# The linear factor of a cubic moved from VectorE to GpSimd, behind a wait, in an attention and rational-activation kernel

## The chip, the cores and the metric

One core of a Trainium2 chip. The metric is the device time of one execution in microseconds (us); three executions of the kernel before took 319.7, 320.22 and 322.7 us, the median is 320.22 us. Its engines are named as in the profile: PE is the matrix engine (PEld its weight loads), DVE is VectorE, ACT is ScalarE, POOL is GpSimd, SP issues DMAs.

## The reference

Two stages. The first is an attention with features of a polynomial sketch (4 batches, 4 heads, 1088 tokens, head width 32, 8 sketch rows); the second is a layer with a rational activation, from 128 to 2048 and back to 128, over all 4352 tokens.

```
def phi(x):                       # 8 x 8 = 64 features of each token
    a = einsum('rd,bhsd->bhsr', S1, x);  b = einsum('rd,bhsd->bhsr', S2, x)
    return einsum('bhsi,bhsj->bhsij', a, b).reshape(..., 64)
kv = einsum('bhsf,bhsd->bhfd', phi(k), v);   z = sum over s of phi(k)
x  = (phi(q) @ kv) / (phi(q) . z + 1e-6)     # heads joined: 4352 x 128

h = x @ w_in                                  # 4352 x 2048
P = a[0] + a[1]*h + a[2]*h*h + a[3]*h*h*h     # the cubic
Q = 1 + |b[0]|*|h| + |b[1]|*h*h
out = (P / (Q + 1e-6)) @ w_out                # 4352 x 128, float32
```

## The kernel before, in words

The attention of batch 0 begins by itself (lines 447 to 475); the rest of the attention is cut into tasks (lines 488 to 498), and one task is mixed into each step of the main loop (line 527) until the last query piece is done. A task is the keys of one batch (class Keys) or a piece of up to 256 tokens of queries (class Queries: transposes, sketches, copies, features, products, quotient, back, keep). Keys and queries use PE, a copy on ACT, and on DVE the features (an operand in PSUM, lines 203, 276 and 279), the quotient (lines 294 to 297) and transposes.

The activation works on units (lines 322 to 332): 512 tokens by 4 blocks of 128 hidden columns, that is a tile of 128 x 2048; the first two units are 256 tokens by 8 blocks, the last two are half as wide (128 x 1024). There are 35 units, NU. For unit i, with h in bf16 as hh:

- PE: hidden(i, 0) and hidden(i, 1), line 356, four float32 products each into a PSUM tile h_ps (two buffers)
- ACT: evac(i, 0) and evac(i, 1), line 364, PSUM to hh (four buffers)
- DVE: d_abs, u = |hh| by a mask (line 368); d_w, w = |b1|*u + |b0| (line 373, a scaling); d_y, y = w*u (line 378, a product); d_p, p = a3*hh + a2 (line 382, a scaling: the linear factor of the cubic)
- ACT: a_ln, ln = Ln(y + 1 + 1e-6) (line 387); a_exp, r = Exp(-ln) = 1/Q (line 391)
- DVE: d_s, s = hh*r (line 395); d_hs, hs = hh*s (line 399); d_g, g = p*hs (line 403): three products
- PE: gather, line 421, adds r, s and g times three copies of w_out (one scaled by a[0], one by a[1], one plain) in PSUM; so out = a0*r + a1*s + g, times w_out
- store, line 432, when a chunk of tokens is complete: a DVE transpose of PSUM, then DMAs on SP's queue

Nothing reorders the work: the kernel is under a manual schedule, and each engine does its instructions in the order in which the loop writes them; tiles carry the waits between engines. Step i of the loop works on several units at once: hidden and evac on unit i + 2, d_abs, d_w, d_y and d_p on unit i, a_ln and a_exp on unit i - 1, d_s, d_hs and d_g on unit i - 2, gather on unit i - 3, store on unit i - 4. In step i VectorE's order before is (lines 540 to 568):

```
s(i-2), u(i), store's transpose, hs(i-2), key and query features,
w(i), g(i-2), more key features, y(i), p(i), quotient, transposes of the next task
```

GpSimd has no instruction in the loop: it sets constants at the start (lines 116 to 128) and makes the plain bf16 copy of w_out (line 523).

Of the kernel before, what the change touches and what calls it, by code (L numbers as in the profile page):

```python
# [14 lines left out]
AX = mybir.AluOpType  # L15
# [5 lines left out]
def kernel(  # L21
# [13 lines left out]
    nc = tc.nc  # L35
# [23 lines left out]
    mid = ctx.enter_context(tc.tile_pool(name="mid", bufs=2))  # L59
    late = ctx.enter_context(tc.tile_pool(name="late", bufs=3))  # L60
# [77 lines left out]
    for i in range(2):  # L138
        nc.vector.tensor_mul(out=S12[:, :, i, :],
                             in0=sT[i][:, None, 0:R].broadcast_to([128, H, R]),  # L140
# [11 lines left out]
    ab0, ab1 = b_abs[:, 0:1], b_abs[:, 1:2]  # L152
    a2, a3 = a_sb[:, 2:3], a_sb[:, 3:4]
# [179 lines left out]
    live = [dict() for _ in range(NU)]  # L333
    outs = {}

    def ok(i):
        return 0 <= i < NU

    def width(i):
        return units[i][1] * units[i][3]  # L340

    def new(i, key, pool, dt=BF, bufs=None):
        kw = {} if bufs is None else {"bufs": bufs}
        t = pool.tile([128, UW], dt, name=key, **kw)[:, 0:width(i)]
        live[i][key] = t
        return t

    def hidden(i, part):
        if not ok(i) or part * HW >= width(i):
            return  # L350
        t0, tl, f0, per = units[i]
        assert ready[0] >= t0 + tl
        t = live[i]["h", part] = wide()
        for x in range(HW // tl):
            f = f0 + part * (HW // tl) + x
            nc.tensor.matmul(t[:, x * tl:(x + 1) * tl], lhsT=w_in_sb[:, f * 128:(f + 1) * 128],  # L356
                             rhs=xT[:, t0:t0 + tl], start=True, stop=True)

    def evac(i, part):
        if not ok(i) or part * HW >= width(i):  # L360
            return
        if part == 0:
            new(i, "hh", late, bufs=4)
        nc.scalar.copy(out=live[i]["hh"][:, part * HW:(part + 1) * HW], in_=live[i]["h", part])  # L364

    def d_abs(i):
        if ok(i):
            nc.vector.tensor_scalar(out=new(i, "u", mid, bufs=1).bitcast(U16), in0=live[i]["hh"].bitcast(U16),  # L368
                                    scalar1=0x7FFF, scalar2=None, op0=AX.bitwise_and)

    def d_w(i):
        if ok(i):
            nc.vector.tensor_scalar(out=new(i, "w", mid, bufs=1), in0=live[i]["u"], scalar1=ab1, scalar2=ab0,  # L373
                                    op0=AX.mult, op1=AX.add)

    def d_y(i):
        if ok(i):
            nc.vector.tensor_mul(out=new(i, "y", mid), in0=live[i]["w"], in1=live[i]["u"])  # L378

    def d_p(i):  # L380
        if ok(i):
            nc.vector.tensor_scalar(out=new(i, "p", mid), in0=live[i]["hh"], scalar1=a3, scalar2=a2,  # L382
                                    op0=AX.mult, op1=AX.add)

    def a_ln(i):
        if ok(i):
            nc.scalar.activation(out=new(i, "ln", mid, FP, bufs=1), in_=live[i]["y"], func=ACT.Ln, bias=1.0 + 1e-6)  # L387

    def a_exp(i):
        if ok(i):  # L390
            nc.scalar.activation(out=new(i, "r", late), in_=live[i]["ln"], func=ACT.Exp, scale=-1.0)  # L391

    def d_s(i):
        if ok(i):
            nc.vector.tensor_mul(out=new(i, "s", late), in0=live[i]["hh"], in1=live[i]["r"])  # L395

    def d_hs(i):
        if ok(i):
            nc.vector.tensor_mul(out=new(i, "hs", mid, bufs=1), in0=live[i]["hh"], in1=live[i]["s"])  # L399

    def d_g(i):
        if ok(i):
            nc.vector.tensor_mul(out=new(i, "g", late), in0=live[i]["p"], in1=live[i]["hs"])  # L403
# [3 lines left out]
    def gather(i, part):  # L407

        if not ok(i):
            return  # L410
        t0, tl, f0, per = units[i]
        if f0 == 0 and part == 0:
            pool = att if t0 >= n_tok - 3 * TC else ops
            outs[t0] = pool.tile([128, TC], FP, name="att_ps" if pool is att else "out_ps")
        order = [(x, y) for x in range(per) for y in range(3)]
        if i == NU - 1:
            order = [(x, y) for y in range(3) for x in range(per)]
        n = len(order)
        for x, y in order[n * part // 4:n * (part + 1) // 4]:
            f = f0 + x  # L420
            nc.tensor.matmul(outs[t0][:, :tl], lhsT=w_sb[y][:, f, :],  # L421
                             rhs=live[i][KEYS[y]][:, x * tl:(x + 1) * tl],
                             start=(f == 0 and y == 0), stop=(i == NU - 1 or units[i + 1][0] != t0) and (x, y) == order[-1])

    def store(i):
        if not ok(i):
            return
        t0, tl, f0, per = units[i]
        if f0 + per < nf:
            return  # L430
        o = mid.tile([128, TC], FP, name="out_sb")
        nc.vector.transpose(out=o[:, :tl], in_=outs[t0][:, :tl])
        c = t0
        while c < t0 + tl:
            b = c // S
            ce = min(t0 + tl, (b + 1) * S)
            o_b = out[b * S:(b + 1) * S, :].rearrange("(g j) d -> g j d", g=32)
            j0, j1 = (c - b * S) // 32, (ce - b * S) // 32
            for e in range(d_model // 32):
                eng = nc.scalar if i == NU - 1 and e % 2 else nc.sync  # L440
                eng.dma_start(
                    out=o_b[:, j0:j1, e * 32:(e + 1) * 32],
                    in_=o[e * 32:(e + 1) * 32, c - t0:ce - t0].rearrange("p (j d) -> p j d", d=32))
            c = ce
# [36 lines left out]
    def fetch(b):  # L481
        fetched[b] = (load_k(b), load_v(b), load_q(b))
# [19 lines left out]
    def get_keys(b):  # L502
        if b is None:
            return Nothing()
        if b not in keys:
            keys[b] = Keys(b, fetched[b][0], fetched[b][1])
        return keys[b]

    def get_queries(bx):
        if bx is None:  # L510
            return Nothing()
        if bx not in pieces:
            b, x = bx
            pieces[bx] = Queries(b, fetched[b][2] if b else q0, cuts[x], cuts[x + 1])
        return pieces[bx]

    def weights():
        nc.scalar.activation(out=b_abs, in_=b_sb, func=ACT.Abs)
        for f in range(0, nf, 4):
            for y in range(2):  # L520
                nc.vector.tensor_scalar(out=w_sb[y][:, f:f + 4], in0=w_out_sb_f[:, f:f + 4],
                                        scalar1=a_sb[:, y:y + 1], scalar2=None, op0=AX.mult)
            nc.gpsimd.tensor_copy(out=w_sb[2][:, f:f + 4], in_=w_out_sb_f[:, f:f + 4])
# [3 lines left out]
    for i in range(-2, NU + 4):  # L527
        kb, kc, qx = tasks.get(i, none)
        KB, KC, Q = get_keys(kb), get_keys(kc), get_queries(qx)
        P = get_queries(tasks.get(i - 1, none)[2])  # L530
        if i in fetch_at:
            fetch(fetch_at[i])

        KC.products((0, 1))
        KB.sketches(0)
        KB.sketches(1)
        Q.sketches()

        a_ln(i - 1)
        d_s(i - 2)  # L540
        d_abs(i)
        KC.keep()
        KB.copies(0)
        KB.copies(1)
        Q.copies()
        store(i - 4)
        hidden(i + 2, 0)
        P.back()
        d_hs(i - 2)
        KB.features(0)  # L550
        Q.features()
        d_w(i)
        a_exp(i - 1)
        P.keep()
        hidden(i + 2, 1)
        d_g(i - 2)
        KB.features(1)
        Q.products()
        d_y(i)
        evac(i + 2, 0)  # L560
        for part in range(4):
            gather(i - 3, part)
        evac(i + 2, 1)
        d_p(i)
        Q.quotient()
        nk, _, nq = tasks.get(i + 1, none)
        get_keys(nk).transposes()
        get_queries(nq).transposes()
        if i == -1:
            weights()  # L570
# [31 lines left out]
```

## Time and profile before

| | before |
|---|---|
| median of three executions | 320.22 us (319.7 to 322.7) |
| the profiled execution's own time | 322.05 us |
| its span, first to last instruction | 320.1 us, 3822 instructions |
| PE busy | 286.5 us, 90% |
| PEld busy | 152.6 us, 48% |
| DVE busy | 282.3 us, 88% |
| ACT busy | 216.2 us, 68% |
| POOL busy | 4.2 us, 1%, 24 instructions |
| DMA | 11.29 MB, 35 GB/s over the span |
| mean granted clock of PE | 0.962 |

The profile is of one execution. Busy time is the union of an engine's instructions; instructions of one engine can overlap by some hundredths of a us at their ends, so what one costs in a row of many is read from start to start. In a row of groups stand line, engine, operation, what is written and read with its shape, the count, the busy time and the mean in ns, then the idle time ahead of them and what ended it. A row of stages gives start and end, the length, and then busy time and count. The chain of work that ended last is followed back from the last instruction to what released each.

### The profile page before, as it was taken

What the parts mean: (1) busy time and instruction counts of PE and PEld (TensorE: products, weight loads), DVE (VectorE), ACT (ScalarE), POOL (GpSimd) and SP (SyncE); (2) the same over time, 40 slices, a digit from 0 to 9 for tenths busy, and PEclk for the clock granted to TensorE, in tenths of its full rate; (3) what the DMA queues carried; (4) which work ended last, traced back from release to release, by engine and by line L of the source; (5) the groups of instructions that cost most, each with busy time, mean ns of one, the idle gap of its engine ahead of it and who ended that gap; (6) DMA issues with size and microseconds to landing.
All of it is one profiled execution on the core that took longest, in us unless ns stands there. A gap on an engine that the chain in (4) does not pass through costs nothing.

```text
span 320.1 us, 3822 instructions
## 1 busy us (share of the span) xinstructions
PE 286.5 (90%) x1420; PEld 152.6 (48%) x1420; DVE 282.3 (88%) x410; ACT 216.2 (68%) x226; POOL 4.2 (1%) x24
## 2 busy tenths in 40 slices
PE   0969769979999999999999999999999899995763
PEld 0857635646655555554565555444433343342221
DVE  2430299799999999999999999999999999999992
ACT  1123454877786688778667778887888878887450
POOL 2020000000000000000000000000000000000000
PEclk9996997979999999999999999999999999999589
DMA  5894020000080002000100001001000100200202
GB/s 176 281 257 112 0 73 0 0 3 0 15 212 1 2 0 33 3 0 0 31 3 2 0 9 25 2 0 32 3 2 4 28 0 0 33 2 0 33 1 33
DMA packets 24626, 11.29 MB, mean 35 GB/s; under 512 B 20384, under 2 KB 22432, under 8 KB 24608
## 3 DMA queue, kind: packets, MB, share of 16 engines
q1 hardware_dynamic: 22832, 10.62, 13.5%
q10 hardware_dynamic: 1776, 0.43, 0.7%
q8 instruction: 11, 0.18, 0.2%
q14 instruction: 7, 0.06, 0.1%
HBM read 8.82 MB, written 2.23 MB: 35 GB/s over the span
## 4 chain that ended last, share of the span: by engine, by line
PE 70%; DVE 21%; issue 4%; ACT 3%; DMA 1%; ACTq 0%; DVEq 0%
PE h_ps L356 31%; PE out_ps L421 17%; PE att_ps L260 6%; PE att_ps L286 5%; DVE g L403 4%; PE att_ps L226 4%; DVE s L395 3%; DVE hs L399 3%; PE att_ps L421 3%; PE att_ps L186 2%; DVE y L378 2%; DVE p L382 2%; DVE u L368 2%; DVE w L373 1%; DMA s_raw<-in_S_dram 1%
## 5 line engine op out<-in xcount | busy, mean ns | idle before, releaser
L356 PE MATMUL h_ps<-xT,w_in_sb 128*128 128x512 f32 (+1 forms) x288 | 133.2, 598 | 3.6 <-ACT hh L364 3.6
L387 ACT ACTIVATE ln<-y 128x2048 f32<-128x2048 bf16 (+1 forms) x35 | 65.3, 1864 | 26.3 <-DVE y L378 26.2
L356 PEld LDWEIGHTS h_ps<-xT,w_in_sb 128*128 128x128 f32 x288 | 53.1, 198 | 54.0 <-issue 42.3
L364 ACT CAST hh<-h_ps 128x1024 bf16<-128x1024 f32 x68 | 67.8, 1013 | 12.9 <-PE h_ps L356 11.7
L421 PEld LDWEIGHTS <-w_out 128*128 128x128 bf16 x432 | 43.1, 101 | 60.7 <-issue 24.2
L391 ACT ACTIVATE r<-ln 128x2048 bf16<-128x2048 f32 (+1 forms) x35 | 65.4, 1868 | 0.5
L403 DVE TENSOR_TENSOR g<-p,hs 128x2048 bf16<-128x2048 bf16 (+1 forms) x35 | 41.4, 1183 | 0.2
L378 DVE TENSOR_TENSOR y<-w,u 128x2048 bf16<-128x2048 bf16 (+1 forms) x35 | 41.4, 1182 | 0.0
L399 DVE TENSOR_TENSOR hs<-hh,s 128x2048 bf16<-128x2048 bf16 (+1 forms) x35 | 41.1, 1175 | 0.1
L395 DVE TENSOR_TENSOR s<-hh,r 128x2048 bf16<-128x2048 bf16 (+1 forms) x35 | 40.8, 1166 | 0.0
L421 PE MATMUL out_ps<-r,w_out 128*128 128x512 bf16 (+1 forms) x96 | 34.7, 362 | 0.0
L421 PE MATMUL out_ps<-s,w_out 128*128 128x512 bf16 (+1 forms) x96 | 34.7, 361 | 0.0
L421 PE MATMUL out_ps<-g,w_out 128*128 128x512 bf16 (+1 forms) x96 | 34.7, 361 | 0.0
L382 DVE TENSOR_SCALAR p<-hh,a_sb 128x2048 bf16<-128x2048 bf16 (+1 forms) x35 | 27.5, 787 | 0.0
L373 DVE TENSOR_SCALAR w<-u,b_abs 128x2048 bf16<-128x2048 bf16 (+1 forms) x35 | 27.5, 785 | 0.0
L421 PE MATMUL att_ps<-g,w_out 128*128 128x512 bf16 x48 | 19.6, 411 | 7.6 <-DVE g L403 7.6
L270 ACT COPY a_sk<-att_ps 128x256 f32<-128x256 f32 (+1 forms) x36 | 10.4, 340 | 22.4 <-PE att_ps L260 22.4
L260 PE MATMUL att_ps<-qT,SAB 64*128 64x256 f32 (+1 forms) x144 | 19.7, 393 | 4.3 <-DVE qT L247 4.3
L368 DVE TENSOR_SCALAR u<-hh 128x2048 uint16<-128x2048 uint16 (+1 forms) x35 | 23.2, 664 | 0.0
L286 PEld LDWEIGHTS att_ps<-kvz,q_pT 128*128 128x128 f32 (+1 forms) x144 | 17.9, 185 | 10.8 <-issue 5.4
L421 PE MATMUL att_ps<-s,w_out 128*128 128x512 bf16 x48 | 19.7, 414 | 0.5 <-DVE s L395 0.5
L421 PE MATMUL att_ps<-r,w_out 128*128 128x512 bf16 x48 | 19.8, 416 | 0.0
(48 smaller groups left out, 176.2 us busy)
## 6 DMA issues: line engine op xcount, KB each, us to landing
k_sb<-in_k_dram SPq DMA_DIRECT2D x4, 544.0 KB, 5.4
v_sb<-in_v_dram SPq DMA_DIRECT2D x16, 128.0 KB, 5.1
q_sb<-in_q_dram SPq DMA_DIRECT2D x3, 544.0 KB, 4.6
out_dram<-out_sb SPq DMA_DIRECT2D x18, 64.0 KB, 2.0
w_in_sb<-in_moe_w_in_dram SPq DMA_DIRECT2D x4, 256.0 KB, 4.0
q_sb<-in_q_dram SPq DMA_DIRECT2D x1, 288.0 KB, 4.0
q_sb<-in_q_dram ACTq DMA_DIRECT2D x1, 256.0 KB, 4.8
out_dram<-out_sb SPq DMA_DIRECT2D x4, 56.0 KB, 1.9
```

Source lines behind the costliest of these rows:

```text
L260: nc.tensor.matmul(self.sk[hp][:, i], lhsT=SAB[i][p, :], rhs=self.qT[p, :n], start=True, stop=True)
L286: nc.tensor.matmul(self.nd[:self.tl, o:o + 2 * KW], lhsT=self.q_p[:, c, t * self.tl:(t + 1) * self.tl], rhs=kvz[self.b % 2][:, c, :], star ...
L356: nc.tensor.matmul(t[:, x * tl:(x + 1) * tl], lhsT=w_in_sb[:, f * 128:(f + 1) * 128], rhs=xT[:, t0:t0 + tl], start=True, stop=True)
L364: nc.scalar.copy(out=live[i]["hh"][:, part * HW:(part + 1) * HW], in_=live[i]["h", part])
L378: nc.vector.tensor_mul(out=new(i, "y", mid), in0=live[i]["w"], in1=live[i]["u"])
L382: nc.vector.tensor_scalar(out=new(i, "p", mid), in0=live[i]["hh"], scalar1=a3, scalar2=a2, op0=AX.mult, op1=AX.add)
L387: nc.scalar.activation(out=new(i, "ln", mid, FP, bufs=1), in_=live[i]["y"], func=ACT.Ln, bias=1.0 + 1e-6)
L391: nc.scalar.activation(out=new(i, "r", late), in_=live[i]["ln"], func=ACT.Exp, scale=-1.0)
L395: nc.vector.tensor_mul(out=new(i, "s", late), in0=live[i]["hh"], in1=live[i]["r"])
L399: nc.vector.tensor_mul(out=new(i, "hs", mid, bufs=1), in0=live[i]["hh"], in1=live[i]["s"])
L403: nc.vector.tensor_mul(out=new(i, "g", late), in0=live[i]["p"], in1=live[i]["hs"])
L421: nc.tensor.matmul(outs[t0][:, :tl], lhsT=w_sb[y][:, f, :], rhs=live[i][KEYS[y]][:, x * tl:(x + 1) * tl], start=(f == 0 and y == 0), stop= ...
```

## The change

p is made on GpSimd and no longer on VectorE. It goes to the pool with three buffers (late) and not to that with two (mid). A dependency is added by hand: p(i) waits until w(i) is done, the second of VectorE's two scalings in the step that are left (u and w). VectorE's order in a step is written anew:

```
u(i), w(i), s(i-2), y(i), store's transpose, key and query features,
hs(i-2), g(i-2), more key features, quotient, transposes of the next task
```

The orders of PE and ACT stay as they were. What is computed is the same.

```diff
     def d_w(i):
         if ok(i):
-            nc.vector.tensor_scalar(out=new(i, "w", mid, bufs=1), in0=live[i]["u"], scalar1=ab1, scalar2=ab0,
-                                    op0=AX.mult, op1=AX.add)
+            live[i]["w_made"] = nc.vector.tensor_scalar(
+                out=new(i, "w", mid, bufs=1), in0=live[i]["u"], scalar1=ab1, scalar2=ab0,
+                op0=AX.mult, op1=AX.add)
...
     def d_p(i):
         if ok(i):
-            nc.vector.tensor_scalar(out=new(i, "p", mid), in0=live[i]["hh"], scalar1=a3, scalar2=a2,
-                                    op0=AX.mult, op1=AX.add)
+            made = nc.gpsimd.tensor_scalar(out=new(i, "p", late), in0=live[i]["hh"], scalar1=a3, scalar2=a2,
+                                           op0=AX.mult, op1=AX.add)
+
+            tc.add_manual_dep(made.ins, live[i]["w_made"].ins.name,
+                              mybir.DependencyInfo(mybir.DependencyClass.Sync, mybir.DependencyReason.DATA),
+                              reason="after the scalings")
...
         a_ln(i - 1)
+        d_abs(i)
+        d_w(i)
+        d_p(i)
         d_s(i - 2)
-        d_abs(i)
+        d_y(i)
         KC.keep()
...
         P.back()
-        d_hs(i - 2)
         KB.features(0)
         Q.features()
-        d_w(i)
+        d_hs(i - 2)
         a_exp(i - 1)
...
         Q.products()
-        d_y(i)
         evac(i + 2, 0)
         for part in range(4):
             gather(i - 3, part)
         evac(i + 2, 1)
-        d_p(i)
         Q.quotient()
```

## The prediction

> **What bounds the kernel now.** I read the busy times by stage first, then the chain of work that ended last, then the order of VectorE's instructions in the late stage, and last what GpSimd has done at all. The stages (us, then busy time and count of PE, PEld, DVE, ACT, POOL, then clock, DMA share, GB/s):
>
> ```profile
> 43.50:66.30 22.80, 18.17 (x133) 10.77 (x131) 20.27 (x35) 17.11 (x22) 0.00 (x0) 0.93 0.00 1
> 66.30:204.70 138.40, 138.38 (x763) 76.23 (x764) 136.60 (x212) 104.31 (x121) 0.00 (x0) 0.99 0.09 20
> 204.70:234.90 30.20, 30.20 (x101) 13.19 (x100) 30.20 (x33) 25.60 (x20) 0.00 (x0) 1.00 0.06 9
> 234.90:308.50 73.60, 62.09 (x200) 25.23 (x199) 73.60 (x83) 56.59 (x40) 0.00 (x0) 0.95 0.07 11
> ```
>
> Up to 204.7 us, where the attention pieces are still mixed in, PE is full, and DVE idles only 138.40 - 136.60 = 1.80 us. From 234.9 us on DVE is full and PE has holes. The chain of work that ended last says the same; its start times give PE's period:
>
> ```profile
> 172.23 1.06 PE att_ps L260 x8
> ...
> 177.99 2.59 PE out_ps L421 x12
> 180.58 1.06 PE att_ps L260 x8
> ...
> 211.21 3.43 PE h_ps L356 x8
> 214.64 2.59 PE out_ps L421 x12
> 217.23 3.43 PE h_ps L356 x8
> ```
>
> A step with a query piece takes 180.58 - 172.23 = 8.35 us, a step without one 217.23 - 211.21 = 6.02 us on PE. DVE's turn of the late stage, in order of time (start, duration):
>
> ```profile
> 256.41 1.21 DVE L378 TENSOR_TENSOR y<-w,u 128x2048 bf16<-128x2048 bf16 x1
> 257.55 0.80 DVE L382 TENSOR_SCALAR p<-hh,a_sb 128x2048 bf16<-128x2048 bf16 x1
> 258.27 1.21 DVE L395 TENSOR_TENSOR s<-hh,r 128x2048 bf16<-128x2048 bf16 x1
> 259.41 0.68 DVE L368 TENSOR_SCALAR u<-hh 128x2048 uint16<-128x2048 uint16 x1
> 260.01 1.21 DVE L399 TENSOR_TENSOR hs<-hh,s 128x2048 bf16<-128x2048 bf16 x1
> 261.14 0.80 DVE L373 TENSOR_SCALAR w<-u,b_abs 128x2048 bf16<-128x2048 bf16 x1
> 261.87 1.21 DVE L403 TENSOR_TENSOR g<-p,hs 128x2048 bf16<-128x2048 bf16 x1
> 263.00 1.21 DVE L378 TENSOR_TENSOR y<-w,u 128x2048 bf16<-128x2048 bf16 x1
> ```
>
> The turn is 263.00 - 256.41 = 6.59 us, longer than PE's 6.02: so PE waits. From start to start p costs 258.27 - 257.55 = 0.72, u 0.60, w 0.73, and each of the products y, s, hs, g 1.13 to 1.14 us. I count in these, since one instruction's end overlaps the next one's start. DVE is the bound late and tied with PE before: whatever lengthens DVE's turn lengthens the kernel in every step, while what shortens it pays only late.
>
> **What is removed.** p leaves VectorE. Its instructions, and its share of the time after 204.7 us; then DVE's busy time in that same stretch:
>
> ```profile
> L382 DVE TENSOR_SCALAR p<-hh,a_sb 128x2048 bf16<-128x2048 bf16 x33 | 26.5, 802 | 0.0
> L382 DVE TENSOR_SCALAR p<-hh,a_sb 128x1024 bf16<-128x1024 bf16 x2 | 1.1, 531 | 0.0
> 303.88 0.46 DVE p L382
> 204.70:313.90 109.20, 12.27 (x16) 0.95 0.06 10
> 204.70:313.90 109.20, 108.86 (x122) 0.95 0.06 10
> ```
>
> Over all steps 33 x 0.72 + 2 x 0.46 = 24.7 us come off DVE. Where PE is full that buys nothing. After 204.7 us there are 16 (14 wide, 2 half): 14 x 0.72 + 2 x 0.46 = 11.0 us, and DVE has 0.34 us of idle time there, so that is the whole possible gain. PE caps it little: DVE's turn would be 6.59 - 0.72 = 5.87 against PE's 6.02, 0.15 us in each of some 13 steps, 2 us.
>
> **What is added.** GpSimd gets 35 p. After 21.7 us it does nothing now, and no DMA of the loop is on its queue, so behind a waiting p stands only the next p. Its price is not in the trace; the nearest rows are these:
>
> ```profile
> L523 POOL CAST w_out<-w_out_sb_f 128x512 bf16<-128x512 f32 x4 | 2.3, 612 | 16.7 <-DMA w_out_sb_f<-in_moe_w_out_dram 16.7
> L122 POOL MEMSET v_sb<- 128x128 f32 x2 | 0.4, 212 | 0.1
> L586 POOL MEMSET const-float32-0.0<- 128x1 f32 x1 | 0.1, 98 | 0.2 <-issue 0.2
> masks.py:199 POOL TENSOR_SCALAR_AFFINE_SELECT ident<-ident 128x128 f32<-128x128 f32 x1 | 0.3, 292 | 0.1
> ```
>
> One element takes 98 ns; from there the memset rises by (212 - 98)/127 = 0.90 ns an element, the cast by (612 - 98)/511 = 1.01, the select by 1.53. For 2048 elements that is 1.94, 2.16 and 3.2 us. I take the cast, which like p reads a tensor and writes bf16: 2.16 us, 1.13 for a half step. As work of GpSimd this is hidden: p(i) is needed by g(i) two steps later, more than 11 us, and it has a third buffer. The cost is what it does to VectorE meanwhile.
>
> **The term that decides: products beside a GpSimd that reads.** From its wait on w, p runs beside s and y. Each reads two tensors of 4 KB a partition in 1.13 us, 7.2 bytes a ns; u reads one in 0.60 us, 6.8 bytes a ns. So the products draw on SBUF as fast as the scalings which p is made to avoid: nothing in the trace says that they leave a path free. The one DVE instruction that ran beside GpSimd's cast (19.41 to 21.69 us) is the second of these:
>
> ```profile
> 15.75 0.69 DVE L276 TENSOR_TENSOR q_pT<-h_ps,a_sk 128x512 f32<-128x512 f32 x1 [2.07 <-ACT a_sk L267]
> 19.41 2.28 POOL L523 CAST w_out<-w_out_sb_f 128x512 bf16<-128x512 f32 x4 [16.70 <-DMA w_out_sb_f<-in_moe_w_out_dram]
> 20.33 0.69 DVE L276 TENSOR_TENSOR q_pT<-h_ps,a_sk 128x512 f32<-128x512 f32 x1 [0.83 <-ACT a_sk L267]
> ```
>
> It was not slowed (0.69 both times), but one of its operands is in PSUM; none of the four products has one there. So the bounds are: nothing, or the whole of p. I take the whole: a product waits while p reads, or p waits until VectorE pauses and then holds it up, which costs the same. [...]
>
> Added to DVE: 33 x 2.16 + 2 x 1.13 = 73.5; removed 24.7; net +48.8. DVE's idle time takes up 22.80 - 20.27 = 2.53 before 66.3 us, 1.80 and 0.34 after: 4.7. Left +44.1. With the memset's slope p is 0.22 us shorter, 7.5 us in all: +36.6. What could hide more is work that reads one operand from PSUM, the features of queries and keys (43.5 to 313.9 us):
>
> ```profile
> 43.50:313.90 270.40, 10.35 (x32) 0.97 0.07 14
> 43.50:313.90 270.40, 8.26 (x9) 0.97 0.07 14
> ```
>
> at most 10.35 + 8.26 = 18.6 us. They come after s and y, 2.27 us behind w, when p should be over, so I count little of it. **I take +40 us.** The profiled execution (322.05 us, its span 320.1 and 1.9 around it) would become 362; the median of the runs stands 1.8 lower, so **360 us**.
>
> **What is moved, at nothing.** In the new order hs ends 0.60 + 0.73 + 1.14 + 1.14 + 1.21 = 4.8 us into a step (counted from its first VectorE instruction), before it was 261.22 - 258.27 = 2.95. The evacuation into hh four buffers on must wait for it. ACT's late turn:
>
> ```profile
> 257.72 1.91 ACT L387 ACTIVATE ln<-y 128x2048 f32<-128x2048 bf16 x1 [0.92 <-DVE y L378]
> 259.66 1.91 ACT L391 ACTIVATE r<-ln 128x2048 bf16<-128x2048 f32 x1
> 261.48 1.91 ACT L364 CAST hh<-h_ps 128x1024 bf16<-128x1024 f32 x2
> 264.31 1.91 ACT L387 ACTIVATE ln<-y 128x2048 f32<-128x2048 bf16 x1 [0.92 <-DVE y L378]
> ```
>
> ACT works 264.31 - 257.72 - 0.92 = 5.67 us of 6.59, and y now ends 0.60 + 0.73 + 1.14 + 1.21 = 3.7 us into the step instead of 264.21 - 258.27 = 5.9, so ln no longer waits. PE's next use of that PSUM buffer lies behind the 2.59 us of gathering. If this cover failed, 1.85 - 0.92 = 0.9 us a step would show, 14 us over the last 16 steps. Query features start 3.6 us into the step instead of 2.9, and store's transpose later too; 24.7 us of relief on DVE covers both.
>
> **Rivals.** (1) GpSimd and the products do not disturb each other; the scalings alone would, and p avoids them. For it: the undisturbed q_pT; against it: that row's PSUM operand and the equal reading rates. Then p is free, PE bounds until 204.7 us, and the gain is the 11.0 us: 322.05 - 11.0 - 1.8 = 309 us (307 to 313). The deciding point is whether s and y keep 1.13 us from start to start. [...] (2) Half: products and p take turns, so DVE loses half of p: 36.8 - 24.7 - 4.7 = +7.4, 328 us (323 to 340). (3) Only the bytes count: p's 4 KB at 7.2 bytes a ns are 0.57 us against 0.72 removed, a gain of 0.15 us in 16 steps, 2.4 us: 318. (4) p is slow as the select was: 3.2 us, 34 x 1.04 = 35 us on top of the sum: about 399. (5) The change doesn't do what it says: GpSimd gets no turn during the run of products, p(i) comes late and g waits for it, DVE idles. The price is that of the forecast, only the row differs, so it has no chance of its own.
>
> **How the numbers follow.** Forecast 0.48, rival 1 0.29, rival 2 0.13, rival 3 0.05, rival 4 0.05. The forecast's own range is 345 to 375 (features hide up to 15 of their 18.6 us, or p is dearer by up to as much). The range over the cases, 307 to 372, leaves out rival 4 and the forecast's upper end. About 1%, 3 us, is what can be told from no change: faster is rival 1, 0.29; same is rival 3, 0.05; slower is the forecast with rivals 2 and 4, 0.66.
>
> **What would show it.** Right: the L382 group is on POOL, about 2.2 us each or longer; one product of a step (s or y) takes over 2 us, or stands behind a gap that p ends, or g waits for p; DVE's late turn is about 8 us, the query steps about 9.7; PE has holes everywhere. Wrong: all four products at 1.2 us, no waits for POOL, late period 6.0 us, PE full until about 283 us. A sum that is wrong in size shows in p's duration alone. If ACT's hh waits for hs in most late steps, the moved hs was not free.

## The result, and the profile after

The changed kernel takes 347.44 us (median of 4 executions, 342.76 to 350.75) against 321.46 us (4 executions); the ratio is 1.076, with a 95% interval of 1.063 to 1.090: slower by 7.6%. The ratio leaves out the execution of 350.75 us, which was in a slower state at a lower granted clock (0.934), so it lies below the quotient of the two medians, 1.081. The forecast was 360 us, slower, with a range of 307 to 372.

The executions differ by some us in when their main loop begins, so I also count the loop alone, from the start of u of unit 2 to that of u of unit 34, 32 steps later. Before (in order of time: start, duration):

```profile
56.54 0.68 DVE L368 TENSOR_SCALAR u<-hh 128x2048 uint16<-128x2048 uint16 x1
...
305.40 0.41 DVE L368 TENSOR_SCALAR u<-hh 128x1024 uint16<-128x1024 uint16 x1
```

and after:

```profile
52.30 0.64 DVE L368 TENSOR_SCALAR u<-hh 128x2048 uint16<-128x2048 uint16 x1
...
323.52 0.42 DVE L368 TENSOR_SCALAR u<-hh 128x1024 uint16<-128x1024 uint16 x1
```

That is 305.40 - 56.54 = 248.9 us before and 323.52 - 52.30 = 271.2 us after: +22.4 us.

The profile page's shares of the chain that ended last, after, by engine: before it was PE 70% and DVE 21%, now they have changed places.

```profile
DVE 70%; PE 21%; issue 5%; DMA 2%; DVEq 0%; ACT 0%; ACTq 0%
```

The stage from 66.3 us on, after (as in the prediction: length, then busy time and count of PE, PEld, DVE, ACT, POOL). PE, which was full to 204.7 us, has holes there too:

```profile
66.30:204.70 138.40, 130.91 (x722) 72.70 (x728) 134.30 (x185) 95.75 (x113) 57.91 (x16) 0.99 0.09 19
```

The groups by line, shapes kept apart (count, busy time, mean ns, idle time ahead of them). The two products that were made first, s and y, are as they were; hs and g have grown from 1205 and 1213 ns to 1806 and 1739:

```profile
L383 POOL TENSOR_SCALAR p<-hh,a_sb 128x2048 bf16<-128x2048 bf16 x33 | 138.5, 4198 | 156.0 <-DVE w L373 140.9 <-ACT ln L392 9.9 <-ACT a_sk L270 5.3
L404 DVE TENSOR_TENSOR hs<-hh,s 128x2048 bf16<-128x2048 bf16 x33 | 59.6, 1806 | 0.0
L408 DVE TENSOR_TENSOR g<-p,hs 128x2048 bf16<-128x2048 bf16 x33 | 57.4, 1739 | 3.6
L379 DVE TENSOR_TENSOR y<-w,u 128x2048 bf16<-128x2048 bf16 x33 | 40.2, 1219 | 0.1
L400 DVE TENSOR_TENSOR s<-hh,r 128x2048 bf16<-128x2048 bf16 x33 | 40.2, 1218 | 0.0
```

A mean of 1.8 us is a mixture; the order of time shows what happens. A late turn (DVE and POOL):

```profile
271.80 0.81 DVE L373 TENSOR_SCALAR w<-u,b_abs 128x2048 bf16<-128x2048 bf16 x1
272.53 1.22 DVE L400 TENSOR_TENSOR s<-hh,r 128x2048 bf16<-128x2048 bf16 x1
272.81 4.96 POOL L383 TENSOR_SCALAR p<-hh,a_sb 128x2048 bf16<-128x2048 bf16 x1 [2.72 <-DVE w L373]
273.67 1.22 DVE L379 TENSOR_TENSOR y<-w,u 128x2048 bf16<-128x2048 bf16 x1
274.80 1.22 DVE L404 TENSOR_TENSOR hs<-hh,s 128x2048 bf16<-128x2048 bf16 x1
276.15 2.70 DVE L408 TENSOR_TENSOR g<-p,hs 128x2048 bf16<-128x2048 bf16 x1
...
279.49 0.81 DVE L373 TENSOR_SCALAR w<-u,b_abs 128x2048 bf16<-128x2048 bf16 x1
```

p's row is 4.96 us long, and y and hs run beside it undisturbed, one right after the other. Then comes a pause of 0.13 us (hs ends at 276.02, g needs it and starts at 276.15), and g takes 2.70 us: it ends at 278.85, 1.08 after p's end at 277.77. So I read p's row as mostly waiting: where its work begins is in no row. It got its turn at the pause, worked for 277.77 - 276.02 = 1.75 us, and g stood until p was done, 2.70 - 1.22 = 1.48 us longer than undisturbed. The turn is 279.49 - 271.80 = 7.69 us, before 6.59. A query step:

```profile
183.31 0.81 DVE L373 TENSOR_SCALAR w<-u,b_abs 128x2048 bf16<-128x2048 bf16 x1
184.03 1.22 DVE L400 TENSOR_TENSOR s<-hh,r 128x2048 bf16<-128x2048 bf16 x1
184.32 3.91 POOL L383 TENSOR_SCALAR p<-hh,a_sb 128x2048 bf16<-128x2048 bf16 x1 [5.15 <-DVE w L373]
185.17 1.22 DVE L379 TENSOR_TENSOR y<-w,u 128x2048 bf16<-128x2048 bf16 x1
186.30 0.75 DVE L279 TENSOR_TENSOR q_pT<-att_ps,a_sk 128x256 f32<-128x256 f32 x2
186.97 2.33 DVE L404 TENSOR_TENSOR hs<-hh,s 128x2048 bf16<-128x2048 bf16 x1
...
192.36 0.81 DVE L373 TENSOR_SCALAR w<-u,b_abs 128x2048 bf16<-128x2048 bf16 x1
```

Here p gets in when the features q_pT begin, which have an operand in PSUM, and works from y's end at 186.39 to 188.23, 1.84 us. q_pT takes the time that it took before (0.75 us, 0.74 before); hs, behind it, waits 1.1 us. The step is 192.36 - 183.31 = 9.05 us, before 8.35.

### The profile page after: what moved, and what is told of

It reads as the page before. It is cut to its first block, busy times and chain, and to the rows that moved or that the text cites. A ratio compares the mean times of both kernels' runs of the same rounds, so it can differ in the third digit from the quotient of the medians.

```text
span 341.0 us, 3854 instructions
## 1 busy us (share of the span) xinstructions
PE 285.7 (84%) x1405; PEld 151.0 (44%) x1420; DVE 300.2 (88%) x375; ACT 213.5 (63%) x226; POOL 148.8 (44%) x59
## 4 chain that ended last, share of the span: by engine, by line
DVE 70%; PE 21%; issue 5%; DMA 2%; DVEq 0%; ACT 0%; ACTq 0%
DVE hs L404 16%; DVE g L408 15%; DVE y L379 10%; DVE s L400 9%; PE h_ps L356 8%; DVE u L368 5%; DVE w L373 5%; PE att_ps L226 3%; DVE q_pT L279 2%; DVE x_tok L297 2%; PE att_ps L426 2%; PE att_ps L286 2%; DMA s_raw<-in_S_dram 2%; PE att_ps L260 1%; DVE out_sb L437 1%
## 5 line engine op out<-in xcount | busy, mean ns | idle before, releaser
L383 POOL TENSOR_SCALAR p<-hh,a_sb 128x2048 bf16<-128x2048 bf16 (+1 forms) x35 | 144.6, 4132 | 161.8 <-DVE w L373 146.6
L364 ACT CAST hh<-h_ps 128x1024 bf16<-128x1024 f32 x68 | 66.0, 1015 | 69.6 <-DVE hs L404 61.7
L356 PEld LDWEIGHTS h_ps<-xT,w_in_sb 128*128 128x128 f32 x288 | 52.1, 195 | 65.5 <-issue 42.0
L408 DVE TENSOR_TENSOR g<-p,hs 128x2048 bf16<-128x2048 bf16 (+1 forms) x35 | 58.8, 1679 | 3.9
L404 DVE TENSOR_TENSOR hs<-hh,s 128x2048 bf16<-128x2048 bf16 (+1 forms) x35 | 61.0, 1742 | 0.1
L426 PE MATMUL out_ps<-r,w_out 128*128 128x512 bf16 (+1 forms) x86 | 30.9, 359 | 2.4 <-DVE out_sb L437 2.4
L260 PE MATMUL att_ps<-qT,SAB 64*128 64x256 f32 (+1 forms) x144 | 18.5, 373 | 7.5 <-DVE qT L247 7.4
L286 PE MATMUL att_ps<-kvz,q_pT 128*128 128x66 f32 (+1 forms) x144 | 18.2, 266 | 1.5 <-DVE q_pT L276 1.0
L426 PE MATMUL att_ps<-s,w_out 128*128 128x512 bf16 x45 | 18.7, 418 | 0.1
```

Source lines behind the costliest of these rows:

```text
L286: nc.tensor.matmul(self.nd[:self.tl, o:o + 2 * KW], lhsT=self.q_p[:, c, t * self.tl:(t + 1) * self.tl], rhs=kvz[self.b % 2][:, c, :], star ...
L383: made = nc.gpsimd.tensor_scalar(out=new(i, "p", late), in0=live[i]["hh"], scalar1=a3, scalar2=a2, op0=AX.mult, op1=AX.add)
L426: nc.tensor.matmul(outs[t0][:, :tl], lhsT=w_sb[y][:, f, :], rhs=live[i][KEYS[y]][:, x * tl:(x + 1) * tl], start=(f == 0 and y == 0), stop= ...
```

## The experiments

Theory A: p on GpSimd doesn't get its turn while VectorE makes one product after another. It gets it at the first pause or at the first instruction with an operand in PSUM, and then the next product waits until p is done, 1.75 to 1.93 us. Rivals: the new order costs the time (B), any work of GpSimd does, writing too (C), GpSimd gets in at any boundary or shares (D), each change of hands has a fixed price (F), a p on GpSimd costs more than it takes off wherever it stands (G), a p that is not kept off the scalings is dearer yet (the idea behind the wait).

| run | ratio to before (95%) or median | u of unit 2, of unit 34 | loop against before | u of unit 3, loop from there against before |
|---|---|---|---|---|
| changed kernel | 1.076 (1.063 to 1.090) | 52.30, 323.52 | +22.4 | 61.76, +23.5 |
| order alone | 1.014 (1.004 to 1.023) | 53.18, 307.46 | +5.4 | 62.04, +7.2 |
| constant for p | 312.4 us (before 320.0) | 55.17, 295.44 | -8.6 | 66.21, -9.0 |
| no wait | 1.077 (1.067 to 1.087) | 57.00, 331.96 | +26.1 | 69.65, +24.0 |
| products spaced | 1.047 (1.039 to 1.055) | 55.82, 320.70 | +16.0 | 66.88, +15.6 |
| half of p | 1.004 (0.999 to 1.008) | 51.55, 299.13 | -1.3 | 61.01, -0.2 |
| engine alone | 1.038 (1.029 to 1.048) | 57.74, 318.80 | +12.2 | 70.55, +10.0 |
| GpSimd in query steps only | 1.004 (0.999 to 1.009) | 53.15, 301.85 | -0.2 | 64.28, -0.7 |
| spaced, all on VectorE | 1.013 (1.007 to 1.019) | 56.75, 306.50 | +0.9 | 68.77, -0.5 |

The loop columns compare single traced executions. The step from unit 2 to unit 3 still belongs to the start-up: it took 10.59 us before, 9.46 in the changed kernel and 8.86 to 12.81 in the others. The last column leaves it out (before, u of unit 3 starts at 67.13); where the two columns differ, this one step makes the difference.

**The new order alone.**

```diff
-            made = nc.gpsimd.tensor_scalar(out=new(i, "p", late), ...)
-            tc.add_manual_dep(made.ins, live[i]["w_made"].ins.name, ...)
+            nc.vector.tensor_scalar(out=new(i, "p", late), ...)
```

> p back on VectorE, at its new place after w; the rest of the new order stays. Theory A (a p on GpSimd gets its turn at the first pause of VectorE and then keeps the next product waiting until it is done): the loss is p's own, so the late turn is VectorE's work, 6.59 us plus the new pauses between dependent neighbours (u to w 0.1, hs to g 0.2), 6.9 us, and the time about 324 us. Rival B (the new order itself costs what was lost: hs late, evacuation late, pauses): about 345 us still.

A late turn of it:

```profile
259.44 0.69 DVE L368 TENSOR_SCALAR u<-hh 128x2048 uint16<-128x2048 uint16 x1
260.16 0.81 DVE L373 TENSOR_SCALAR w<-u,b_abs 128x2048 bf16<-128x2048 bf16 x1
...
263.88 1.22 DVE L400 TENSOR_TENSOR hs<-hh,s 128x2048 bf16<-128x2048 bf16 x1
265.20 1.23 DVE L404 TENSOR_TENSOR g<-p,hs 128x2048 bf16<-128x2048 bf16 x1
266.35 0.69 DVE L368 TENSOR_SCALAR u<-hh 128x2048 uint16<-128x2048 uint16 x1
```

The turn is 266.35 - 259.44 = 6.91 us: w stands 0.72 us behind u (0.60 before), g 1.32 behind hs (1.13), because each now follows the instruction that it needs. A query step takes 8.60 us, before 8.35. The time is 1.4% over before (0.4 to 2.3%). Rival B falls as the cause of the whole, but the order has a price of its own, 5.4 us of the loop's 22.4 (from unit 3 on 7.2 of 23.5), that the prediction didn't have.

The prediction named a sign for a moved hs that isn't free: ACT's hh waits for hs in most late steps. That sign came. The evacuations before, and in this run (count, busy time, mean ns, idle time ahead of them):

```profile
L364 ACT CAST hh<-h_ps 128x1024 bf16<-128x1024 f32 x68 | 67.8, 1013 | 12.9 <-PE h_ps L356 11.7 <-DVE hs L399 1.2
L364 ACT CAST hh<-h_ps 128x1024 bf16<-128x1024 f32 x68 | 66.0, 1015 | 57.2 <-DVE hs L400 51.6 <-PE h_ps L356 4.1 <-PE out_ps L422 1.5
```

ACT waits 51.6 us for hs, but VectorE doesn't wait for ACT: its view of waits has no entry from 204.7 to 300 us, so what lengthens its late turn by 0.32 us is the two pauses.

**A constant for p.** GpSimd writes p and reads nothing; the linear factor is left out.

```diff
-            made = nc.gpsimd.tensor_scalar(out=new(i, "p", late), in0=live[i]["hh"], ...)
+            made = nc.gpsimd.memset(new(i, "p", late), 0.5)
```

> GpSimd writes a constant into p after w instead of computing it; the linear factor is left out of the computation. GpSimd then writes as much as before and reads nothing. Theory A with the contention on reading: no product waits, all four stay at 1.2 us, the late turn is 5.87 plus 0.3 of pauses, 6.2 us, and the time about 314 us: that is the price of rival 1 of the prediction. Rival C (any work of GpSimd beside VectorE, writing too, holds a product up): a product still takes over 2 us, late turn 7.7 us, about 345 us.

```profile
252.62 0.81 DVE L373 TENSOR_SCALAR w<-u,b_abs 128x2048 bf16<-128x2048 bf16 x1
253.34 1.22 DVE L398 TENSOR_TENSOR s<-hh,r 128x2048 bf16<-128x2048 bf16 x1
253.55 1.81 POOL L383 MEMSET p<- 128x2048 bf16 x1 [4.38 <-DVE w L373]
254.48 1.22 DVE L379 TENSOR_TENSOR y<-w,u 128x2048 bf16<-128x2048 bf16 x1
255.62 1.22 DVE L402 TENSOR_TENSOR hs<-hh,s 128x2048 bf16<-128x2048 bf16 x1
256.96 1.23 DVE L406 TENSOR_TENSOR g<-p,hs 128x2048 bf16<-128x2048 bf16 x1
...
258.83 0.81 DVE L373 TENSOR_SCALAR w<-u,b_abs 128x2048 bf16<-128x2048 bf16 x1
```

GpSimd is busy nearly as long as with a p that waits for nothing (1.81 us; such a row of p takes 2.05 in the next run), begins at once, beside s and y, and nothing waits. The late turn is 258.83 - 252.62 = 6.21 us, the median 312.4 us (307.2 to 313.0; before 319.3 to 323.3). Rival C falls: work of GpSimd that only writes holds no product up, so it is what p has beyond the writing. That is its reading and its arithmetic, and no run separates the two. This is also what rival 1 of the prediction was worth with the new order in it, about 8 to 9 us.

**No wait on w.**

```diff
-            tc.add_manual_dep(made.ins, live[i]["w_made"].ins.name, ...)
```

> The dependency of p on w is taken out, all else as in the changed kernel. p(i) can then start when g(i-3) frees its buffer, at the end of the step before, beside quotient and transposes, which have an operand in PSUM or only one. Theory A: in steps with queries about 1.1 us of p is hidden there (0.7 in the changed kernel), the step is about 8.7 us instead of 9.06; late, p gets in at the pause between u and w and w waits 1.8 us, the late turn stays 7.7 us; in all about 6 us less than the changed kernel. The idea behind the wait (only the scalings disturb GpSimd, so a p beside them costs more): slower than the changed kernel by up to 1 us a step.

Late, and in a query step (DVE and POOL):

```profile
261.77 0.69 DVE L368 TENSOR_SCALAR u<-hh 128x2048 uint16<-128x2048 uint16 x1
262.02 2.35 POOL L383 TENSOR_SCALAR p<-hh,a_sb 128x2048 bf16<-128x2048 bf16 x1 [5.47 <-DVE g L404]
262.49 2.43 DVE L373 TENSOR_SCALAR w<-u,b_abs 128x2048 bf16<-128x2048 bf16 x1
...
186.70 2.05 POOL L383 TENSOR_SCALAR p<-hh,a_sb 128x2048 bf16<-128x2048 bf16 x1 [6.96 <-DVE rec L294]
186.88 0.42 DVE L297 TENSOR_TENSOR x_tok<-att_ps,rec 128x256 f32<-128x256 f32 x1
187.22 0.43 DVE L247 STREAM_TRANSPOSE qT<-q_sb 128x256 f32<-128x256 f32 x1
187.58 1.72 DVE L368 TENSOR_SCALAR u<-hh 128x2048 uint16<-128x2048 uint16 x1
```

The places are those of theory A: late, p gets in at the pause between u and w, and w waits 1.6 us; in a query step it runs beside quotient and transposes, and u waits 1.1. But the forecast of 6 us less was wrong: the ratio is that of the changed kernel, and so is the loop from unit 3 on (+24.0 against +23.5). Beside the quotient p saves nothing over beside the features, since u waits as long as hs did. So the wait on w neither helps nor hurts: it only chooses which VectorE instruction pays.

**No product behind the one it needs.**

```diff
         d_abs(i)
+        d_s(i - 2)
         d_w(i)
         d_p(i)
-        d_s(i - 2)
+        d_hs(i - 2)
         d_y(i)
...
         Q.features()
-        d_hs(i - 2)
```

> The changed kernel with no product right behind the one it needs: VectorE's order is u, s, w, hs, y, transposes and features, g; p still waits for w. Theory A: late, VectorE then has no pause at which GpSimd could get in, so p is starved until g needs it two steps later: p's rows take 7 us or more each, g waits for POOL, and the turn is still 5.87 + 1.85 = 7.7 us; the time is that of the changed kernel within 1%. Rival D (GpSimd gets its turn at any boundary between two VectorE instructions, or shares): p's rows stay near 2 to 4 us and it is another product than g that is long.

```profile
265.19 12.57 POOL L383 TENSOR_SCALAR p<-hh,a_sb 128x2048 bf16<-128x2048 bf16 x1 [3.73 <-DVE w L373]
...
274.79 1.21 DVE L400 TENSOR_TENSOR s<-hh,r 128x2048 bf16<-128x2048 bf16 x1
275.92 2.38 DVE L373 TENSOR_SCALAR w<-u,b_abs 128x2048 bf16<-128x2048 bf16 x1
```

p is starved, as theory A has it: this one stands from 265.19 to 277.76 us while VectorE passes ten boundaries and loses nothing. Another stood for 15.73 us, from 211.81, until g waited for it. But then this one gets in between s and w, where no row shows a pause, another late p got in between g and u (u 2.38 us), and one between two products, y and g (g 2.91 us). Theory A's "at a pause only" is too narrow; what lets GpSimd in at such a boundary, and not at others like it, stays open. The time, 336.5 us, is 3% below the changed kernel; I had expected it within 1%. A query step takes 8.74 us instead of 9.06, which is the 0.3 us of the pauses; a late p still costs 1.6 to 1.7 us.

**Half of p.** The second half of the linear factor is left out; g reads the first half twice.

```diff
-            made = nc.gpsimd.tensor_scalar(out=new(i, "p", late), in0=live[i]["hh"], ...)
+            made = nc.gpsimd.tensor_scalar(out=new(i, "p", late)[:, 0:width(i) // 2],
+                                           in0=live[i]["hh"][:, 0:width(i) // 2], ...)
...
```

> The changed kernel with half of each p: GpSimd makes the first half of its columns and g reads that half twice (the second half of the linear factor is left out). Theory A (the product that waits does so for the whole of p, 1.85 us at full width): p takes 0.95 us at half width, the late turn falls from 7.69 to about 6.75 us, hs in query steps from 2.33 to about 1.3 us, the query step to 8.4 us; about 322 us. Rival F (a fixed price for each change of hands between the two engines): turn and time as in the changed kernel, about 345 us.

```profile
252.15 0.68 DVE L368 TENSOR_SCALAR u<-hh 128x2048 uint16<-128x2048 uint16 x1
...
253.87 4.11 POOL L383 TENSOR_SCALAR p<-hh,a_sb 128x1024 bf16<-128x1024 bf16 x1 [2.72 <-DVE w L373]
...
257.21 1.84 DVE L409 TENSOR_TENSOR g<-p,hs 128x2048 bf16<-128x2048 bf16 x1
258.98 0.68 DVE L368 TENSOR_SCALAR u<-hh 128x2048 uint16<-128x2048 uint16 x1
```

g shrinks from 2.70 to 1.84 us, the turn from 7.69 to 258.98 - 252.15 = 6.83, the median to 319.5 us. The price goes with p's length; rival F falls. Even with half of the factor left out GpSimd's share buys nothing against the kernel before.

**The engine alone: before's order, p on GpSimd.**

```diff
-            nc.vector.tensor_scalar(out=new(i, "p", mid), ...)
+            nc.gpsimd.tensor_scalar(out=new(i, "p", mid), ...)
```

> The kernel before with p on GpSimd and nothing else changed: VectorE's old order, no wait on w. Theory A: in query steps p falls beside quotient and transposes and is mostly hidden, 8.35 us a step as before; late, p costs some VectorE instruction 1.6 to 1.85 us, the turn is 5.87 plus that, 7.5 to 7.7 us against 6.59, over 14 to 16 steps 13 to 18 us: about 335 us, faster than the changed kernel. The idea behind the wait (a p that is not kept off the scalings is dearer): slower than the changed kernel, over 347 us.

333.5 us, as theory A had it, and 14 us less than with the wait and the new order, of which the order alone is 5 to 7. Query steps take 8.39 us, late turns 7.56. Late, p again gets in without a visible pause, between u and hs:

```profile
257.37 4.46 POOL L382 TENSOR_SCALAR p<-hh,a_sb 128x2048 bf16<-128x2048 bf16 x1 [3.10 <-ACT hh L364]
...
259.39 0.68 DVE L368 TENSOR_SCALAR u<-hh 128x2048 uint16<-128x2048 uint16 x1
259.99 2.90 DVE L399 TENSOR_TENSOR hs<-hh,s 128x2048 bf16<-128x2048 bf16 x1
```

**GpSimd in query steps only**, before's order.

```diff
-            nc.vector.tensor_scalar(out=new(i, "p", mid), ...)
+            eng = nc.gpsimd if tasks.get(i, none)[2] is not None else nc.vector
+            eng.tensor_scalar(out=new(i, "p", mid), ...)
```

> The kernel before with p on GpSimd only in the steps that have a query piece, and on VectorE in all others; old order, no wait. Theory A: p runs beside quotient and transposes (1.1 us that need no second SBUF operand), VectorE's turn loses 0.72 and is held up about 0.7 us, PE bounds these steps anyway: 8.35 us a step, the time within 1% of the kernel before. Rival G (a p on GpSimd costs more than it takes off wherever it stands): query steps over 8.6 us, 4 us or more in all, about 325 us.

```profile
181.09 2.89 POOL L383 TENSOR_SCALAR p<-hh,a_sb 128x2048 bf16<-128x2048 bf16 x1 [5.50 <-DVE g L404]
...
183.11 1.93 DVE L396 TENSOR_TENSOR s<-hh,r 128x2048 bf16<-128x2048 bf16 x1
```

1.004 (0.999 to 1.009): the same. p works beside quotient and transposes, s waits 0.7 us where 0.72 was taken off, and a query step takes 8.39 us; rival G falls. Nothing is gained, because there VectorE was not what the kernel waited for (before, PE was busy for 138.38 of the 138.40 us from 66.3 to 204.7, VectorE for 136.60), and late, where it is (before, busy for 73.60 of the 73.60 us from 234.9 to 308.5), it has next to no instruction that leaves GpSimd a turn for nothing. No run that computes the whole of p beats the kernel before.

**Spaced, all on VectorE.** The order of the spaced run, p back on VectorE behind w.

```diff
-            made = nc.gpsimd.tensor_scalar(out=new(i, "p", late), ...)
-            tc.add_manual_dep(made.ins, live[i]["w_made"].ins.name, ...)
+            nc.vector.tensor_scalar(out=new(i, "p", late), ...)
```

> VectorE alone, p not on GpSimd: the order of the run with spaced products (u, s, w, p, hs, y, transposes and features, g). If the 1.4% that the new order alone costs are the pauses between dependent neighbours (u to w 0.1 us, hs to g 0.2 us in a turn), they are gone here: late turn 6.59 us, time within 1% of the kernel before. If they are the late hs and its evacuations, the time stays above 323 us.

```profile
253.93 0.68 DVE L368 TENSOR_SCALAR u<-hh 128x2048 uint16<-128x2048 uint16 x1
...
260.51 0.68 DVE L368 TENSOR_SCALAR u<-hh 128x2048 uint16<-128x2048 uint16 x1
```

The pauses are gone, the turn is 260.51 - 253.93 = 6.58 us, a query step 8.35, and the loop is 0.9 us over before, not 5.4 (from unit 3 on -0.5, not +7.2). This order also brings hs forward, to 4.40 us into the step from 5.66 with the order alone, so the run by itself doesn't separate the pauses from the late evacuations; VectorE's empty view of waits in the run with the order alone does. So the pauses are the loop's part of the order's price. The ratio, 1.013 (1.007 to 1.019), is nevertheless not within 1%; 0.9 us is 0.3%, and where the rest lies, outside of the loop or between executions, is not settled.

## Why the prediction was right, and where it was off

- **What bounds**: right. VectorE was tied with PE to 204.7 us and the bound after it, and every us that was put on its turn lengthened the kernel.
- **The deciding term**: right in kind. One product of a step stands until p is done: g 2.70 us late, hs 2.33 in query steps. Of its two forms it was the second, "p waits until VectorE pauses and then holds it up", where q_pT, with an operand in PSUM, serves p as a pause does, and some boundaries without a pause too. What was concluded from the equal reading rates, that a product fares no better than a scaling, held: g took 2.70 us instead of 1.22, and w, in the run without the wait, 2.43 instead of 0.81. The size, a product held up for the whole of p, 2.16 us in every step, was the author's estimate, which no run shows; the runs showed 1.48 us late and 1.11 in a query step of the changed kernel, and elsewhere, for example, 0.7 (s, GpSimd in query steps only) and 1.7 (hs, the engine alone). Beside a memset of 1.81 us s and y kept their 1.22, so writing alone does no harm, and q_pT takes 0.75 us beside p, 0.74 before. At y and at hs a waiting p was passed over (1.22 us each, late).
- **The sum**: +40 us against 347.44 - 321.46 = 26. The step that failed is "They come after s and y, 2.27 us behind w, when p should be over, so I count little of it". p doesn't begin behind w but behind the run of products, just where the query features (or store's transpose) stand, and these hide 0.7 us of it. So a query step grew by 0.70 us, to 9.05, not to the 9.7 us that the prediction named. From the rows, a query step is 0.72 relieved against 1.11 us of waiting (hs 2.33 instead of 1.22) and 0.3 of pauses, +0.7; a late one 0.72 against 1.48 and 0.3, +1.1, and 7.69 - 6.59 = 1.10 is measured.
- **p's length**: taken as 2.16 us from the cast. The row of a p that waits for nothing is 2.05 us long (186.70, run without the wait), so this was nearly right; what I read as work in the rows of a p that waited is 1.75 to 1.93 us. With that the late turn is 7.69 us and not 5.87 + 2.16 = 8.03, although the pauses are in it.
- **"What is moved, at nothing"**: wrong by 5.4 to 7.2 us of the loop (the run with the order alone). What it missed are not the late evacuations, which it weighed (ACT does wait for hs, as its sign had it, but VectorE doesn't wait for ACT), but two pauses, u to w and hs to g, 0.12 to 0.2 us each, and in the late turn one of them is where p got in. This error and the two above it had opposite signs, so it is in part luck that 347.44 us still lies in the forecast's own range of 345 to 375.
- **Rivals**: (1) falls, its price is about 8 to 9 us by the run with a constant, with the new order's pauses in it; 11 were forecast; (2) and (3), taking turns or sharing bytes, fall, since the products beside p's row keep their 1.22 us and a single one stands until p is done, for a time that shrinks with p (a query step's 1.1 us is half of p only because q_pT covers the rest); (4) falls with p's length; (5) came true in part: in the changed kernel p gets no turn during the run of products, but g's row is longer and VectorE doesn't stand idle; in the spaced run g did wait for a p that had stood for 15.73 us.

Put together from the loops: the order +5.4, p taken off VectorE -8.6 - 5.4 = -14.0 (the run with a constant less that with the order alone), p's computing on GpSimd instead of a constant 22.4 - (-8.6) = +31.0, that is 0.9 us for each of 35 p. From unit 3 on the three are +7.2, -16.2 and +32.5, again 0.9 for each p.

## What to carry to other kernels

In this kernel a p on GpSimd, which reads SBUF, cost nothing beside VectorE instructions with an operand in PSUM (q_pT 0.75 us against 0.74 before, x_tok 0.42 with and without it) and beside the float32 transposes (qT, 0.43 both times). Beside a row of products it mostly waited (p's rows of 3.91 and 4.96 us against 2.05), and then one product, or one scaling, waited for p. So price such a move as GpSimd's own time less what VectorE has at that place that isn't disturbed, and not as what VectorE is relieved of: here 1.1 us held up in a query step and 1.5 in a late one, for 0.72 relieved. And when reordering one engine, look for instructions that come to stand right behind what they need: each cost a pause of 0.12 to 0.2 us here, and in the changed kernel's late turn such a pause is where GpSimd got in.

## What the runs showed of the hardware that was not expected

- A busy row of GpSimd contains its wait for VectorE: p's rows were 3.91, 4.96 and up to 15.73 us long, where a p that waits for nothing has 2.05; half of the work took 0.86 us off the waiting product (g 1.84 instead of 2.70).
- A p that waits is mostly passed over between two products that follow each other without a pause (s and y, y and hs, late in the changed kernel, 1.22 us each). It was let in at some boundaries where no pause shows, in front of w, u or hs (2.38, 2.38 and 2.90 us), and in the spaced run in front of g right behind y (g 2.91 us); by what rule is open.
- The scalings, with one operand in SBUF, suffer like the products: in the run without the wait w took 2.43 us behind u when p got in between (0.81 undisturbed), and u 1.72 (0.65).
- Neighbours on VectorE of which the second needs the first stand 0.12 to 0.2 us further apart (0.72 against 0.60 us, 1.32 against 1.13).
